# Two attention passes over one cache: lists of three early units in place of four, two units moved to each end, three rereads of a weight in place of four

## The chip, the cores and the metric

The kernel runs on one core of one Trainium2 chip. The metric is the device time of one launch in microseconds (us), the median over runs. Lower is better.

## The reference

Two blocks are applied one after the other, twice, to a decode step of eight rows (one token each), with the same weights and the same K and V caches both times:

```python
x = A_x
x = x + _A_ref(_layernorm(x), A_k_cache, A_v_cache, A_wq, A_wo)
x = x + _B_ref(_layernorm(x), B_w1, B_w2, B_w3, B_w4)
x = x + _A_ref(_layernorm(x), A_k_cache, A_v_cache, A_wq, A_wo)
x = x + _B_ref(_layernorm(x), B_w1, B_w2, B_w3, B_w4)

def _A_ref(x, k_cache, v_cache, wq, wo):      # B=8, D=448, 16 query heads, 8 kv heads, Sk=4096, Dh=256
    q = (x @ wq).reshape(B, Sq, Hq, Dh)
    scores = einsum("bhqd,bhkd->bhqk", q, repeat(k_cache, 2)) * Dh ** -0.5
    return einsum("bhqk,bhkd->bhqd", softmax(scores), repeat(v_cache, 2)).reshape(B, Sq, Hq * Dh) @ wo
```

With one token per row, the mixer inside `_B_ref` shifts everything out of the sequence, so of B there remain the norms, the two matrices w3 and w4 with a gelu between them, and the sums.

The caches are bf16, 128 MiB each. Everything else is small beside them.

## The kernel before

**Units, tiles and places.** The work of one pass, one row and one pair of kv heads is a unit, written (pass, row, pair): pass 0 or 1, rows 0 to 7, pairs 0 to 3. A unit has four K tiles and four V tiles of 1 MiB each. Tiles are loaded into 17 places of 1 MiB in SBUF. A K tile is turned in place by VectorE (three STREAM_TRANSPOSE, `transpose_k`, L897), then TensorE multiplies it with the query (`scores`, L904). Two tiles that lie in neighbouring places can be scored by one series of 256-wide matmuls (`also`), otherwise each has a series of 128-wide ones. A V tile needs 16 matmuls (`pv`, L978).

**What is read once and what twice.** Pairs 2 and 3 (`keep`) are "kept": once a row's pass 0 has used their tiles, they stay in the places, PSUM and a spare tile until the row's pass 1 has used them too. Pairs 0 and 1 (`free`) are read from HBM in each pass. Each row therefore has two free units in pass 0 and two in pass 1, 32 in all.

**Chains and lists.** Between a row's two passes lies a chain of small dependent steps (`chain`, L550): the output of pairs 2 and 3 times wo, norm, w3, gelu, w4, norm, the query of pass 1. While it runs, nearly all places hold the row's kept tiles, and three are left. To have something to do meanwhile, the plan takes free units of later rows out of their order (`ahead`, L624 to L628): their K tiles are turned and scored before the chain, and their V tiles are used under it. These V items are called `narrow`; the first twelve of a list are `halved`, that is, loaded as two DMAs of 512 KiB. A list has four units in rows 0, 1, 2 and 7 and three in rows 3 to 6. Row 0's own two free units of pass 0 come at the start (L700, L701), row 7's two of pass 1 at the end (L712, L713).

**The order.** `block`, `weights` and `first_kept` (L642 to L697) write the whole order of work by hand as a list of items: 527 of them, K (0), V (1) or weight (2). Within `block`, V items that are due are put between the K items. The main loop (L1113) walks the items. At each it issues the engines' work, then gives free places back and issues the next loads (`emit_loads`, L824) in the order of the items, on SyncE's queue, as far as places are free. Two K tiles of a `paired` unit (L744) are loaded by one 2 MiB DMA when two neighbouring places are free in time (`both_for`, L794).

**Generators.** The chain and the smaller jobs are Python generators that `step` (L1047) moves on by one yield at each item: of each of the kinds "chain", "last" and "rest", the oldest. While a chain runs under its narrow items (`alone`), other generators of the kinds "chain" and "last" wait. When a unit's output is complete, `half` (L504) scales it, copies it out of its PSUM bank, clears the bank and turns it into columns. There are two such banks (`free_o`). In pass 0 a row's pairs 0 and 1 go through one `half` (`first_half`, L545, kind "chain"); in pass 1 through `last` (L585, kind "last"), one for each unit if the two lie in different lists (`split`).

**Weights that are read again.** Half of wq (the heads of pairs 0 and 1) and half of wo have no lasting place. The wq half, 1.75 MiB in two places, is read at the start for all rows of pass 0 and then for pass 1 of the rows (0,3), (3,5), (5,7) and (7,8) (`q_rows`, L630). On its arrival TensorE makes the queries of those rows (`project_rows`, 64 matmuls, L350) and VectorE copies them. The wo half, 896 KiB, is read five times (`o_rows`, L631); `early_rows` (L599) multiplies the finished outputs of pairs 0 and 1 by it and adds the result to x. It first forces generators on until these outputs are there. At the last wo, `rest` does the second block of rows 0 to 3 for pass 1; rows 4 to 7 follow after the last V tile.

Of the kernel before, what the change touches and what calls it, by code (L numbers as in the profile page):

```python
# [17 lines left out]
def kernel(  # L18
# [521 lines left out]
    turned = {}  # L540

    def told(ps, b, gps):
        turned[ps, b] = turned.get((ps, b), 0) + len(gps)
# [55 lines left out]
    def early_rows(r0, r1, ps, slot):  # L599

        nb = r1 - r0
        for r in range(r0, r1):
            while turned.get((ps, r), 0) < (2, 4)[ps]:
                step(10 * len(items))
        y_ps = misc[:, 400 : 400 + 4 * nb].rearrange("p (f b) -> p f b", b=nb)
        run(
            add_cols(
                y_ps,
                lambda i: OT2[:, i % 2, i // 2, r0:r1],
                lambda i, at: wo_of(i, at, slot),  # L610
                range(NB2 // 2),
                4,
            )
        )
        xs = xT[:, :, r0:r1]
        nc.vector.tensor_add(xs, xs, y_ps)
# [15 lines left out]
    split = {  # L632
        (1, b)
        for b in range(Bn - 1)
        if any(sum((1, b, gp) in units for gp in free) == 1 for units in ahead)
# [6 lines left out]
    def block(k, v=None):  # L642

        fresh = [(number[v], 1, c) for c in range(4)] if v else []
        if k is None:
            due.extend(fresh)
            items.extend(due)
            due.clear()
            return
        number[k] = len(tasks)  # L650
        tasks.append(k)
        two = k[0] == 1 and k[2] in keep
        for c in range(4):
            items.append((number[k], 0, c))
            if two and c % 2 == 0:
                continue
            items.extend(due[:1])
            del due[:1]
            if c <= two:
                due.extend(fresh)  # L660
# [41 lines left out]
    o_rows[0] = (0, 1)  # L702
    first_kept(0, ahead[0], (0, 0, free[1]))
    for b in range(Bn):
# [39 lines left out]
    def paired(n, c):  # L744

        ps, _, gp = tasks[n]
        return gp in keep or tasks[n] in saved
# [365 lines left out]
    for idx, it in enumerate(items):  # L1113
# [10 lines left out]
        ps, b, gp = tasks[n]  # L1124
        if it == kept_q:
# [8 lines left out]
        if kv == 2:  # L1134
            rows = b
            if gp == "o" and rows is None:
                end_wo = slot
            elif gp == "o":
                early_rows(*rows, 0, slot)
                if rows[1] == Bn:  # L1140
                    assert pairs_done[1, MID - 1] == 4
                    early_rows(0, MID, 1, slot)
                    add_gen("rest", rest(), idx + 1, idx + 18, 20)
            elif c == 1:
# [3 lines left out]
                def q_of_block(c, fc):  # L1148
# [10 lines left out]
                    else misc[:, 352 : 352 + 2 * HH * nb]  # L1159
# [49 lines left out]
        else:  # L1209
# [12 lines left out]
            if final and gp in free:  # L1222
                pv_cols(oc, slot, c, gp, psv[slot_of[n]])
                if c % 2 == 1:
# [3 lines left out]
                    h0 = 8 * gp + 4 * u  # L1228
                    run(
# [9 lines left out]
            else:  # L1239
                g8 = gp // 2  # L1240
                if ("o", g8) not in st:
# [7 lines left out]
                if c == 0 and (alone_now or pairs_done.get((ps, b), 0) % 2 == 1):  # L1249
                    done = pairs_done[ps, b] + 1  # L1250

                    def ready(k=(ps, b), done=done):
                        return pairs_done[k] >= done

                    if ps == 0:
                        g = (first_half if done == 2 else chain)(b, st, ready)
                        add_gen("chain", g, main=done == 4)
# [196 lines left out]
```

## Time and profile before

| | |
|---|---|
| median of 3 runs | 1065.47 us (1064.1 to 1067.35) |
| the profiled execution | 1061.72 us |
| its span, first to last instruction | 1059.6 us |
| moved by DMA | 426.11 MB |
| busy: TensorE, VectorE, ScalarE, GpSimd | 59%, 58%, 15%, 2% of the span |

The profile is of one execution. Its page gives the busy time of each engine, the span in 40 slices, the DMA queues, the chain of work that ended last, groups of instructions by source line, and the DMA issues. Views of the trace cut out stretches of the span ("windows") or list the instructions in order of time; windows give, after the busy times, the granted clock, the busy share of the 16 DMA engines and the GB/s they moved. SPq is SyncE's DMA queue. In names such as `places<-places,qbd`, the left side is written and the right side read.

### The profile page before, as it was taken

The numbers are of one execution on the slowest core, as the hardware profiler recorded it, in microseconds if no ns is written. First come the engines' busy times: TensorE is split into PE (matmuls) and PEld (weight loads), VectorE is DVE, ScalarE is ACT, GpSimd is POOL, SyncE is SP. The second block draws the span as 40 slices with busy tenths as digits, with TensorE's granted clock in tenths as the row PEclk, the third lists the DMA queues.
The fourth block names the chain that finished last, engine by engine and source line by source line (L and its number), as shares of the span: only waits on it lengthen the run. The fifth ranks groups of instructions, "written<-read, shape, count | busy, mean of one in ns | idle before, by whom it ended". The sixth has DMA issues, their size and how long they took to land.

```text
span 1059.6 us, 29163 instructions
## 1 busy us (share of the span) xinstructions
PE 627.0 (59%) x12932; PEld 395.0 (37%) x12932; DVE 616.4 (58%) x1319; ACT 161.7 (15%) x613; POOL 16.4 (2%) x27
## 2 busy tenths in 40 slices
PE   3144457655575547664586566656764666657675
PEld 2022225432343324442343234423442444434455
DVE  5146862578527882467628952785288437792362
ACT  1011110211111111111112111111111111111110
POOL 0000000000000000000000000000000000000000
PEclk9999996665675656657656566656665686556665
DMA  9999999999999999999999999999999999999994
GB/s 300 387 424 424 424 415 388 422 421 423 401 406 426 424 420 404 409 403 424 414 389 426 425 410 410 378 425 412 401 424 423 393 389 420 423 418 348 393 416 203
DMA packets 71757, 426.11 MB, mean 402 GB/s; under 512 B 7496, under 2 KB 13520, under 8 KB 43856
## 3 DMA queue, kind: packets, MB, share of 16 engines
q1 hardware_dynamic: 71440, 424.01, 98.8%
q8 instruction: 101, 1.65, 0.6%
q10 hardware_dynamic: 192, 0.25, 0.1%
q14 instruction: 24, 0.20, 0.0%
HBM read 424.22 MB, written 0.01 MB: 400 GB/s over the span
## 4 chain that ended last, share of the span: by engine, by line
DMA 47%; DVE 24%; PE 21%; ACT 3%; issue 2%; SPq 2%; POOL 1%; DVEq 0%; ACTq 0%
DMA places<-in_A_v_cache_dram 25%; DMA places<-in_A_k_cache_dram 20%; DVE places L902 18%; PE sc L917 9%; PE o L986 7%; ACT p_n L926 2%; PE misc L174 2%; DMA places<-in_A_wq_dram 2%; PE misc L529 1%; DVE store L937 1%; DVE places L944 1%; DVE qbd L376 1%; SPq L193 1%; SPq L870 1%; ACT o_sb L523 1%
## 5 line engine op out<-in xcount | busy, mean ns | idle before, releaser
L902 DVE STREAM_TRANSPOSE places<-places 128x512 uint32<-128x512 uint32 (+1 forms) x576 | 455.5, 854 | 83.0 <-DMA places<-in_A_k_cache_dram 81.0
L917 PE MATMUL sc<-places,qbd 128*8 128x256 bf16 (+1 forms) x5024 | 246.9, 347 | 244.9 <-DVE places L902 236.1
L986 PE MATMUL o<-places,ptw 128*8 128x256 bf16 x3808 | 232.3, 369 | 101.4 <-DMA places<-in_A_v_cache_dram 70.9
L917 PEld LDWEIGHTS <-qbd 128*8 128x8 bf16 x5024 | 130.4, 104 | 327.8 <-DVE places L902 140.1
L986 PEld LDWEIGHTS <-ptw 128*8 128x8 bf16 x3968 | 103.7, 102 | 171.4 <-issue 95.8
L926 ACT ACTIVATE p_n<-sc 128x256 bf16<-128x256 f32 x128 | 95.4, 745 | 395.1 <-PE sc L917 392.4
L1108 ACT COPY ptw<-psv 128x32 bf16<-128x32 bf16 x248 | 52.6, 226 | 173.7 <-PE o L986 161.4
L976 ACT CAST psv<-misc 128x128 bf16<-128x128 f32 x64 | 17.0, 266 | 253.3 <-PE misc L969 253.3
L493 DVE RECIPROCAL rz<-misc 128x8 f32<-128x8 f32 (+1 forms) x35 | 6.7, 191 | 77.4 <-PE misc L490 77.4
L376 DVE CAST qbd<-misc 32x32 bf16<-32x32 f32 x128 | 23.2, 182 | 27.6 <-PE misc L370 26.3
L529 PE MATMUL misc<-R_t,o_sb 128*128 128x8 f32 (+1 forms) x132 | 26.7, 311 | 20.7 <-DVE R_t L515 13.9
L529 PEld LDWEIGHTS misc<-R_t,o_sb 128*128 128x128 f32 x132 | 23.8, 252 | 30.9 <-issue 17.2
L926 ACT ACTIVATION_READ_ACCUMULATOR p_n<-sc 128x1 f32 x128 | 33.8, 264 | 0.0
L174 PEld LDWEIGHTS <-w_sb 128*128 128x128 bf16 x896 | 27.3, 103 | 14.2 <-issue 13.8
L525 DVE MEMSET o<- 128x256 f32 x33 | 9.0, 272 | 35.0 <-PE o L986 31.2
L490 PE MATMUL misc<-zm,one 128*128 128x8 f32 (+1 forms) x70 | 17.1, 317 | 18.9 <-DVE zm L482 17.1
L275 POOL TENSOR_TENSOR t<-t,nhalf 128x2 f32<-128x2 f32 (+2 forms) x18 | 12.0, 670 | 957.7 <-DVE t L296 957.7
L490 PEld LDWEIGHTS misc<-zm,one 128*128 128x128 f32 x70 | 14.1, 251 | 29.1 <-issue 24.9
L969 PEld LDWEIGHTS <-p_n 128*128 128x128 bf16 x256 | 11.9, 105 | 31.6 <-issue 20.0
L969 PE MATMUL misc<-identb,p_n 128*128 128x32 bf16 x256 | 18.0, 190 | 9.3 <-ACT p_n L926 6.8
L937 DVE STREAM_TRANSPOSE store<-places 128x512 uint32<-128x512 uint32 x32 | 19.8, 686 | 0.0
L944 DVE STREAM_TRANSPOSE places<-store 128x512 uint32<-128x512 uint32 x32 | 19.7, 672 | 0.0
(150 smaller groups left out, 350.8 us busy)
## 6 DMA issues: line engine op xcount, KB each, us to landing
places<-in_A_k_cache_dram SPq DMA_DIRECT2D x62, 2048.0 KB, 17.5
places<-in_A_v_cache_dram SPq DMA_DIRECT2D x194, 512.0 KB, 7.2
places<-in_A_v_cache_dram SPq DMA_DIRECT2D x87, 1024.0 KB, 20.7
places<-in_A_k_cache_dram SPq DMA_DIRECT2D x68, 1024.0 KB, 13.3
places<-in_A_wq_dram SPq DMA_DIRECT2D x5, 1024.0 KB
rest<-in_A_v_cache_dram SPq DMA_DIRECT2D x8, 640.0 KB, 19.6
places<-in_A_wo_dram SPq DMA_DIRECT2D x5, 896.0 KB, 19.7
places<-in_A_v_cache_dram SPq DMA_DIRECT2D x8, 384.0 KB, 18.9
```

The source lines that it names most:

```text
L174: nc.tensor.matmul(bass.AP(out.tensor, out.offset, [out.ap[0], (1, WIDE)]), w, x.to_broadcast([128, WIDE]), start=start, stop=stop, skip_g ...
L376: nc.vector.tensor_copy(qbd[32 * a : 32 * a + 32, :, :, a, :], qs.rearrange("p e (f g u h) -> p (e f) u g h", f=2, u=2, h=2)[:, :, u],)
L490: nc.tensor.matmul(z_ps, ones, zm[:], start=True, stop=True)
L529: nc.tensor.matmul(ot_ps[:, j], o_sb[:].rearrange("p (i j) -> p j i", j=2)[:, j], R, start=True, stop=True)
L902: nc.vector.transpose(w, w)
L917: nc.tensor.matmul(sc[32 * k : 32 * k + 8, 128 * (x % 2) : 128 * (x % 2 + nx)], qbd[:, ep, gp % 2].rearrange("p a h -> p (a h)"), v, start ...
L926: nc.scalar.activation(p_sb[:, :, :, 2 * u : 2 * u + 2].rearrange("p t i x -> p x t i"), sc[:, 0:256].rearrange("p (x t i) -> p x t i", x= ...
L937: nc.vector.transpose(store[n][:].bitcast(U32), slot[:].bitcast(U32)[:, 512 * n : 512 * n + 512])
L944: nc.vector.transpose(slot[:].bitcast(U32)[:, 512 * n : 512 * n + 512], store[n][:].bitcast(U32))
L969: nc.tensor.matmul(pt_ps[:, t], p_sb[:, t].rearrange("p i x -> p (i x)"), cols, start=True, stop=True,)
L986: nc.tensor.matmul(o_ps[32 * q : 32 * q + 8, :], ptz[:, at : at + 8], v[:, y * Dh : (y + 1) * Dh] if v2 is None or y < PR else v2[:, (y - ...
L1108: nc.scalar.copy(ptw[:, ring_of[it], :, 6:8], psv[slot_of[it[0]]][:, it[2]])
```

## The change

- Every list has three units. The order of the free units starts with rows 1 to 6 of pass 0 and goes on with rows 0 to 5 of pass 1; 24 units lie in lists.
- Row 7's two free units of pass 0 follow row 0's at the start. Row 6's two of pass 1 stand before row 7's at the end, behind row 7's kept pairs.
- wq is read again for rows (0,4), (4,6) and (6,8). In the row where the list begins with a unit that needs the new queries (`at_once`, row 4), the reread stands ahead of it and the V items between its K items are spread further apart (`slow`).
- wo is still read five times, at rows 0, 1, 3, 5 and the end. `early_rows` now takes a range of heads, so that a row whose two units fell into different lists is served in two calls, the second half from the resident part of wo without a read (`o_late`, rows 2 and 4).
- `first_half` takes one or both units, since lists now split rows 2 and 5 in pass 0 and rows 1 and 4 in pass 1.
- The queries of a reread go to columns 192 and up of the PSUM tile `misc`, which were 352 and up.
- Ahead of the last row's products the program forces "last" generators to their end.

```diff
-    def first_half(b, st, ready):
-
-        yield from half(st["o", 0], st["z"], [0, 1], OT2[:, :, 0:HH, b], ready)
-        told(0, b, [0, 1])
+    def first_half(b, st, gps, ready):
+
+        o = st.pop(("o", 0))
+        yield from half(o, st["z"], gps, OT2[:, :, 4 * gps[0] : 4 * gps[-1] + 4, b], ready)
+        told(0, b, gps)
...
-    def early_rows(r0, r1, ps, slot):
+    def early_rows(h0, h1, r0, r1, ps, slot):
 
         nb = r1 - r0
-        for r in range(r0, r1):
-            while turned.get((ps, r), 0) < (2, 4)[ps]:
-                step(10 * len(items))
+        while not {(ps, r, h // 4) for r in range(r0, r1) for h in range(h0, h1)} <= turned:
+            assert gens
+            step(10 * len(items))
...
-                range(NB2 // 2),
+                range(2 * h0, 2 * h1),
...
-    order = [(0, b, gp) for b in range(1, Bn) for gp in free]
-    order += [(1, b, gp) for b in range(Bn - 1) for gp in free]
-    ahead = []
-    for n in (4, 4, 4, 3, 3, 3, 3, 4):
-        ahead.append(order[:n])
-        del order[:n]
-    assert len(ahead) == Bn and not order
-
-    q_rows = {3: (0, 3), 5: (3, 5), 7: (5, 7), Bn: (Bn - 1, Bn)}
-    o_rows = {1: (1, 3), 3: (3, 7), 7: (7, 8)}
+    ends = (6, 7)
+    order = [(0, b, gp) for b in range(1, Bn - 1) for gp in free]
+    order += [(1, b, gp) for b in range(ends[0]) for gp in free]
+    ahead = [order[3 * b : 3 * b + 3] for b in range(Bn)]
+    assert len(order) == 3 * Bn
+
+    q_rows = {4: (0, 4), 6: (4, 6), Bn: (6, 8)}
+
+    o_rows = {
+        0: [(0, 8, 0, 1), (0, 8, 7, 8)],
+        1: [(0, 4, 1, 3), (4, 8, 1, 2)],
+        3: [(0, 4, 3, 6), (4, 8, 3, 5)],
+        5: [(0, 8, 6, 7)],
+    }
+    o_late = {2: (4, 8, 2, 3), 4: (4, 8, 5, 6)}
...
-            if two and c % 2 == 0:
+            if (two or slow) and c % 2 == 0:
+                if slow and c == 0:
+                    due.extend(fresh)
                 continue
...
-        ready = b < Bn - 1
-        if b in q_rows and not ready:
+        at_once = b in q_rows and todo[0][1] >= q_rows[b][0]
+        if at_once:
+            block(k2, before)
             weights("q", q_rows[b])
-        block(todo.pop(0), before)
-        if b in q_rows and ready:
-            weights("q", q_rows[b])
-        if len(todo) > 2:
-            block(todo.pop(0))
-        if b in o_rows:
-            weights("o", o_rows[b])
-        block(k2)
-        block(todo.pop(0), k2)
-        if todo:
-            block(todo.pop(0))
+            if b in o_late:
+                o_late_at[len(items)] = o_late[b]
+            block(todo.pop(0), k2, True)
+        else:
+            block(todo.pop(0), before)
+            if b in q_rows:
+                weights("q", q_rows[b])
+            if b in o_rows and b:
+                weights("o", o_rows[b])
+            if b in o_late:
+                o_late_at[len(items)] = o_late[b]
+            block(k2)
+            if not b:
+                weights("o", o_rows[b])
+            block(todo.pop(0), k2)
+        while todo:
+            block(todo.pop(0), None, at_once)
...
-    o_rows[0] = (0, 1)
-    first_kept(0, ahead[0], (0, 0, free[1]))
+    block((0, Bn - 1, free[0]), (0, 0, free[1]))
+    block((0, Bn - 1, free[1]), (0, Bn - 1, free[0]))
+    first_kept(0, ahead[0], (0, Bn - 1, free[1]))
...
             weights("q", q_rows[Bn])
-            block((1, b, free[0]), k2)
-            block((1, b, free[1]), (1, b, free[0]))
-            weights("o", None)
-            block(None, (1, b, free[1]))
+            before = k2
+            for k in [(1, r, gp) for r in range(*q_rows[Bn]) for gp in free]:
+                block(k, before)
+                if before == k2:
+                    weights("o", None)
+                before = k
+            block(None, before)
...
-        return gp in keep or tasks[n] in saved
+        return gp in keep or tasks[n] in saved or tasks[n][:2] == (1, ends[0])
...
+        if idx in o_late_at:
+            early_rows(*o_late_at[idx], 0, None)
...
-                    else misc[:, 352 : 352 + 2 * HH * nb]
+                    else misc[:, 192 : 192 + 2 * HH * nb]
...
+                    while any(e["kind"] == "last" for e in gens):
+                        step(10 * len(items))
```

More of the change, by code (lines that the diff above doesn't have):

```diff
@@ L538 @@
     free_o = list(o_banks)
[L540 removed]
+    turned = set()
     def told(ps, b, gps):
[L543 to L548 removed]
+        turned.update((ps, b, gp) for gp in gps)
+    def first_half(b, st, gps, ready):
+        o = st.pop(("o", 0))
+        yield from half(o, st["z"], gps, OT2[:, :, 4 * gps[0] : 4 * gps[-1] + 4, b], ready)
+        told(0, b, gps)
     def chain(b, st, ready):
@@ L621 @@
     assert Bn > 2 and free == [0, 1] and GP == 4
-    order = [(0, b, gp) for b in range(1, Bn) for gp in free]
-    order += [(1, b, gp) for b in range(Bn - 1) for gp in free]
-    ahead = []
-    for n in (4, 4, 4, 3, 3, 3, 3, 4):
-        ahead.append(order[:n])
-        del order[:n]
-    assert len(ahead) == Bn and not order
-    q_rows = {3: (0, 3), 5: (3, 5), 7: (5, 7), Bn: (Bn - 1, Bn)}
-    o_rows = {1: (1, 3), 3: (3, 7), 7: (7, 8)}
+    ends = (6, 7)
[5 more added lines that the diff above has]
+    o_rows = {
[4 rows of a table added]
+    }
+    o_late = {2: (4, 8, 2, 3), 4: (4, 8, 5, 6)}
+    o_late_at = {}
     split = {
-        (1, b)
-        for b in range(Bn - 1)
-        if any(sum((1, b, gp) in units for gp in free) == 1 for units in ahead)
+        (ps, b)
+        for ps in range(2)
+        for b in range(Bn)
+        if any(sum((ps, b, gp) in units for gp in free) == 1 for units in ahead)
     }
@@ L658, in block @@
             del due[:1]
-            if c <= two:
+            if c <= two and not slow:
                 due.extend(fresh)
@@ L1137 @@
                 end_wo = slot
+                early_rows(0, HH, 0, MID, 1, slot)
+                add_gen("rest", rest(), idx + 1, idx + 18, 20)
             elif gp == "o":
[L1139 to L1143, printed above, removed]
+                for who in rows:
+                    early_rows(*who, 0, slot)
             elif c == 1:
@@ L1240 @@
                 g8 = gp // 2
-                if ("o", g8) not in st:
+                if c == 0 and ("o", g8) not in st:
                     while not free_o:
@@ L1249 @@
                 if c == 0 and (alone_now or pairs_done.get((ps, b), 0) % 2 == 1):
-                    done = pairs_done[ps, b] + 1
+                    done = pairs_done.get((ps, b), 0) + 1
                     def ready(k=(ps, b), done=done):
-                        return pairs_done[k] >= done
+                        return pairs_done.get(k, 0) >= done
                     if ps == 0:
-                        g = (first_half if done == 2 else chain)(b, st, ready)
-                        add_gen("chain", g, main=done == 4)
+                        if done == 4:
+                            add_gen("chain", chain(b, st, ready), main=True)
+                        else:
+                            add_gen(
+                                "chain", first_half(b, st, [gp] if alone_now else free, ready)
+                            )
                     elif done == 2:
```

2 lines of the change are left out of this document (1 added, 1 removed).

## The prediction

> **What bounds the kernel now.** First the page: engines, slices, queue.
>
> ```profile
> PE 627.0 (59%) x12932; PEld 395.0 (37%) x12932; DVE 616.4 (58%) x1319; ACT 161.7 (15%) x613; POOL 16.4 (2%) x27
> DMA  9999999999999999999999999999999999999994
> GB/s 300 387 424 424 424 415 388 422 421 423 401 406 426 424 420 404 409 403 424 414 389 426 425 410 410 378 425 412 401 424 423 393 389 420 423 418 348 393 416 203
> DMA packets 71757, 426.11 MB, mean 402 GB/s; under 512 B 7496, under 2 KB 13520, under 8 KB 43856
> ```
>
> No engine is busy for 60% of the span, and the DMA engines are busy in every slice but the last. Slices come back to 424 to 426 GB/s and never go higher: that is the full rate here. So the kernel is bound by its loads, and the question is which bytes go and where the rate sags. 426.11 MB at 424 GB/s would take 1005.0 us of the 1059.6. I then cut windows: two stretches at the full rate, then the eight stages from a list's first V item to the first kept V item of pass 1, row by row.
>
> ```profile
> 55.00:85.00 30.00, 14.96 (x298) 9.09 (x298) 15.71 (x28) 2.91 (x12) 0.00 (x0) 1.00 1.01 426
> 100.00:140.00 40.00, 16.59 (x312) 9.43 (x308) 31.12 (x48) 5.63 (x19) 0.00 (x0) 1.00 1.01 424
> ```
>
> ```profile
> 158.70:209.30 50.60, 36.23 (x728) 23.78 (x731) 19.14 (x63) 7.57 (x32) 1.26 (x2) 0.66 1.02 405
> 284.00:333.40 49.40, 33.11 (x695) 21.81 (x695) 19.18 (x64) 7.53 (x32) 1.25 (x2) 0.71 1.01 406
> 404.40:454.80 50.40, 35.46 (x724) 22.73 (x724) 19.14 (x64) 7.53 (x32) 1.25 (x2) 0.66 1.02 406
> 523.90:563.40 39.50, 30.60 (x592) 18.99 (x595) 11.20 (x50) 6.11 (x25) 1.26 (x2) 0.62 1.01 399
> 626.00:666.00 40.00, 28.11 (x620) 18.61 (x619) 11.28 (x50) 5.87 (x25) 1.25 (x2) 0.71 1.02 405
> 734.00:774.80 40.80, 28.20 (x620) 18.70 (x619) 13.68 (x54) 5.91 (x25) 1.25 (x2) 0.71 1.02 405
> 836.40:876.90 40.50, 27.39 (x652) 19.01 (x651) 11.26 (x50) 5.83 (x25) 1.25 (x2) 0.79 1.01 385
> 960.00:1015.20 55.20, 38.12 (x853) 25.76 (x852) 19.56 (x66) 7.40 (x32) 1.25 (x2) 0.62 0.98 379
> ```
>
> I price a window by what it lost against the full rate: its length times (1 - GB/s / 424). Rows 0 to 7 lose 2.27, 2.10, 2.14, 2.33, 1.79, 1.83, 3.72 and 5.86 us, together 22.0. Lists of four (rows 0 to 2) and of three (rows 3 to 5) lose alike. Rows 6 and 7 stand out; each has a wq reread inside. Next come the four rereads and the K stretches (turning K tiles, ahead of a list's V items) of rows 6 and 7.
>
> ```profile
> 454.00:460.00 6.00, 3.82 (x99) 2.86 (x98) 3.07 (x6) 1.00 (x4) 0.00 (x0) 0.66 1.07 338
> 664.00:680.00 16.00, 10.80 (x241) 6.61 (x234) 10.31 (x18) 3.21 (x14) 0.00 (x0) 0.61 0.98 352
> 864.00:870.00 6.00, 4.30 (x124) 3.22 (x121) 1.62 (x8) 2.17 (x7) 0.00 (x0) 0.97 1.05 346
> ...
> 994.00:1000.00 6.00, 3.40 (x53) 2.11 (x53) 2.45 (x8) 0.80 (x3) 0.00 (x0) 0.50 1.03 318
> ```
>
> ```profile
> 802.10:836.40 34.30, 18.38 (x338) 9.77 (x342) 25.66 (x38) 6.24 (x22) 0.00 (x0) 0.55 1.01 418
> 925.00:960.00 35.00, 22.05 (x450) 13.38 (x454) 28.57 (x49) 6.42 (x24) 0.54 (x1) 0.50 1.00 407
> ```
>
> The rereads lose 1.22, 2.72, 1.10 and 1.50 us beside their bytes; row 6's K stretch loses 0.49 and row 7's 1.40. Why row 7 is late shows on VectorE, in order of time:
>
> ```profile
> 880.41 0.27 DVE L358 CAST qT<-misc 128x16 bf16<-128x16 f32 x2 [5.88 <-PE misc L350]
> ...
> 903.51 0.16 DVE L616 TENSOR_TENSOR xT<-xT,misc 128x4 f32<-128x4 f32 x1 [2.00 <-PE misc L174]
> 905.61 0.17 DVE L616 TENSOR_TENSOR xT<-xT,misc 128x16 f32<-128x16 f32 x1 [1.94 <-PE misc L414]
> ```
>
> ```profile
> 937.64 15.14 DVE L902 STREAM_TRANSPOSE places<-places 128x512 uint32<-128x512 uint32 x20
> ```
>
> Within 26 us it stands idle 9.8 us, for the reread's queries and for two wo products, with 24 K tiles to turn. A K tile costs it 3 transposes, 15.14 / 20 x 3 = 2.27 us, against 2.47 us for 1 MiB of DMA, so over K tiles alone it hardly catches up. The V items start late, give their three places back late, and DMA starves: its busy share is 0.98 in row 7's stage.
>
> **The change, part by part.**
>
> *One reread less.* 1.75 MiB are 1.835 MB, 4.33 us at 424 GB/s; no place or engine has to give anything for it. Its sag goes too, somewhere between 1.10 and 2.72.
>
> *Where the other three fall.* By its order of items, the reread for (0,4) has ten loads out, itself among them, before the next place comes free; I give it the 1.22 of the first row. That for (4,6) has eight, with two K tiles behind it, just like the one at 664 us: 2.72. That for (6,8) is issued under row 7's list as the third one now is under row 6's, so row 7's stage gets row 6's 3.72. Ahead of it row 7 turns 20 K tiles in place of 24, with no reread and no wo product among them, and `rest` comes only at the end: its K stretch gets row 6's 0.49.
>
> *Lists of three.* Lists in rows 0 to 3 now hold units of pass 0, whose outputs queue behind the chain. Today only row 3 is such a list of three: 2.33 each. Rows 4 to 6 get 1.8. Stages, separate rereads and last K stretch are today 22.04 + 1.22 + 2.72 + 1.40 = 27.4, and then 4 x 2.33 + 3 x 1.8 + 3.72 + 1.22 + 2.72 + 0.49 = 22.9. That is 4.5 us, which holds the sag and row 7's lateness; bounds 1.3 (the lateness of 3.2, below, comes back elsewhere) and 6.7 (rows 0 to 3 come down to row 4's 1.79).
>
> *Units at both ends.* 16 MiB move to each end, K and V tiles in turn, so VectorE has 4.9 us for each 2.27. The loads of the weights at the start are as they were. At the end the last eight V tiles come one per 2.47 us, and this stands unchanged behind them:
>
> ```profile
> 1029.74 18.36 DMA places<-in_A_v_cache_dram
> ...
> 1056.37 0.27 DVE places L1419
> ```
>
> From the last landing at 1048.1 to the end of the span are 11.5 us before and after. Row 6's last `half` has to be done by the second of these eight tiles, six tiles (15 us) ahead of the end, and `rest` earlier still.
>
> *What is added.* The instruction lists of the two builds differ by this: 128 wo matmuls more (448 for 320) in ten calls for five; two more `half`; 20 tiles more that are scored alone, since their places aren't neighbours; 11 K loads of 2 MiB fewer and 22 of 1 MiB more.
>
> ```profile
> L917 PE MATMUL sc<-places,qbd 128*8 128x256 bf16 x3168 | 182.0, 386 | 182.6 <-DVE places L902 180.2 <-DVE places L962 1.3 <-DVE zs_t L479 0.6
> L917 PE MATMUL sc<-places,qbd 128*8 128x128 bf16 x1856 | 64.9, 280 | 62.3 <-DVE places L902 55.8 <-ACT p_n L926 5.3 <-DVE zs_t L479 0.5
> L523 ACT COPY o_sb<-o 128x256 f32<-128x256 f32 x33 | 12.7, 384 | 17.8 <-PE o L986 17.6
> 933.77 0.33 SPq L839 DMA_DIRECT2D places<-in_A_k_cache_dram  x1
> ```
>
> Wo: 64 matmuls keep VectorE idle 1.94 to 2.00 us (rows above), so 128 are 3.9. Scores: 640 narrow matmuls at 64.9 / 1856 = 35.0 ns less 320 wide ones at 182.0 / 3168 = 57.4 ns, 4.0 us of TensorE. A `half` holds a copy of 0.38 us and no DMA; I call it 2 us with its matmuls, two are 4 (an estimate). Together 11.9 us if all lay open, nothing if all is hidden. TensorE and VectorE, idle over 40% of the span while DMA isn't, cover it; the present calls lie in stretches that still move 418 to 420 GB/s. So I take a value near nothing, 0.8. Loads: 1 MiB loads run at 426 GB/s (55 to 85 us, where none is paired), paired ones at 424 (100 to 140 us), so nothing; the open bound is SyncE's 0.33 us an issue, 11 x 0.33 = 3.6.
>
> The Trainium skill, "DMA: Bandwidth & Descriptors", section "Anatomy of one DMA — SWDGE (gpsimd) path", speaks against this edit: it fits each DMA with a fixed 2.0 us beside its bytes. By that the 11 additional DMAs would cost 22 us, an estimate from that page, which would end at 1079. The page fits single DMAs on another issue path; the 426 GB/s row has many on the queue and shows no such cost.
>
> *The sum.* 4.3 + 4.5 - 0.8 = 8.0 us. The profiled execution took 1061.72 us, 2.1 more than its span, and should come to 1053.7. It is itself 3.75 below the median of the three runs; the median should go from 1065.47 to **1057.5 us**.
>
> **The rivals.**
>
> *Late V items in the early rows (slower).* Row 7's lateness is worth 5.86 - 1.50 - 2.10 = 2.3 us in its stage and 1.40 - 0.49 = 0.9 ahead of it, 3.2 together. In the changed kernel wo products stand in the K stretches of rows 1 to 5, two calls each in rows 1 and 3, and forced generators ahead of them. If each of these rows starts its V items as late as row 7 does, that is 5 x 3.2 = 16 us, and the time 1065.5 - 8.0 + 16 = 1073.5. It decides from the third such row (8.0 / 3.2 = 2.5). For it: the idle rows at 903 and 905 us. Against: rows 1 and 3 have a wo call now, of 64 matmuls, and their stages run at 406 and 399; a row's two calls there become two of 32, as much in sum; and each row has 20 K tiles to turn at most, with eight V loads between and behind them that give VectorE 8 x 2.47 = 20 us.
>
> *The lateness moves with a reread.* Row 4's or row 6's K stretch behind its reread takes what row 7's loses: 1057.5 + 3.2 = 1060.7. For it: the 5.88 us of idle VectorE. Against: the second reread has such a stretch behind it now, and the stage that follows runs at 405.
>
> *The bytes aren't the bound where they are saved.* If after each list the chain sets the time and loads only fill it, the 4.3 us and the sag come back as waiting for places, and row 7's 3.2 and less remain: about 1063 to 1066. For it: 0.98 at 664 us. Against: the busy share is 1.01 or more in seven of the eight stages.
>
> *More issues cost.* 3.6 us by the bound above: 1061.1. Against: the 426 GB/s.
>
> **How the numbers follow.** A measurement of this kernel can't tell less than about 0.3% from no change, so the borders are 1062.3 and 1068.7. The forecast has 0.60, with a range of its own from 1053 (bounds 6.7 and nothing added) to 1061 (4 of the 11.9 open). The late V items have 0.17; a part of it, with two or three late rows, would be no change. The moved lateness has 0.13, the bytes that don't count 0.08, the issues 0.02. Faster: 0.58 + 0.10 + 0.01 + 0.02 = 0.71. No change: 0.02 + 0.03 + 0.06 + 0.03 = 0.14. Slower 0.15. The range goes from 1051 (1.5 us of the runs' spread below 1053) to 1068, which leaves out most of the late rows.
>
> **What would show it.** Right: 424.3 MB moved; a span with three sags of the reread in place of four; row 7's stage at about 385 GB/s and the one before it at 418; stages of some 40 us at 399 to 406 in all other rows; about 11.5 us from the last V landing to the end. Wrong: stages of rows 1 to 5 below 390 GB/s with a busy share under 1.00, V items that wait for VectorE or an output bank rather than for DMA, or a K stretch under 410 behind the rereads of rows 4 and 6. Should the last V tiles have landed well before their products, the end would be bound by engines and the forecast for another reason too low.

## The result, and the profile after

| | median | runs |
|---|---|---|
| before | 1065.61 us | 10, 1063.77 to 1068.58 |
| changed | 1061.86 us | 10, 1059.44 to 1064.14 |

The ratio is 0.996 (95% interval 0.9948 to 0.9971): 3.75 us or 0.4% faster. The direction and the range held; the forecast gain was 8.0. Both profiled executions take the same time, though: 1061.44 us for the changed kernel (span 1059.3), 1061.72 for the one before. The latter lies below all ten timed runs of its kernel, so it flatters the kernel before by almost the whole gain. Stages of the changed kernel are therefore compared below over several traces, and gains by ratios; the kernel before has only this one trace.

The changed kernel's page: its slices, and what its DMA moved.

```profile
GB/s 303 389 420 424 422 420 420 394 416 423 418 388 416 420 415 332 409 423 419 395 394 420 421 377 410 423 421 404 377 424 422 392 417 422 419 398 392 418 418 187
DMA packets 72768, 424.32 MB, mean 401 GB/s; under 512 B 7608, under 2 KB 13632, under 8 KB 43456
```

The 1.8 MB are gone, but the mean rate has not risen with it: 401 GB/s, where it was 402. One slice stands out, the 16th with 332 GB/s, around 411 us. The windows of the changed kernel, cut as before: its eight stages from a list's first V item to the first kept one of pass 1, rows 0 to 7. (Columns as before: length, busy time of the engines, granted clock, busy share of DMA, GB/s.)

```profile
189.00:228.90 39.90, 27.61 (x592) 18.30 (x593) 13.72 (x54) 5.88 (x25) 1.26 (x2) 0.74 1.02 401
293.20:334.20 41.00, 28.26 (x652) 19.16 (x651) 11.27 (x50) 5.92 (x25) 1.25 (x2) 0.71 1.01 395
398.80:441.50 42.70, 31.19 (x652) 20.47 (x651) 13.68 (x54) 5.95 (x25) 1.25 (x2) 0.58 0.97 361
504.80:545.50 40.70, 28.50 (x592) 18.29 (x595) 11.13 (x50) 5.97 (x25) 1.25 (x2) 0.71 1.01 401
613.00:654.60 41.60, 28.72 (x589) 18.72 (x589) 13.69 (x54) 5.95 (x25) 1.25 (x2) 0.71 1.01 388
718.00:758.00 40.00, 27.65 (x588) 18.34 (x587) 11.27 (x50) 5.92 (x25) 1.25 (x2) 0.75 1.02 404
825.60:867.00 41.40, 28.63 (x624) 19.34 (x627) 13.73 (x54) 5.92 (x25) 1.25 (x2) 0.66 1.02 403
927.40:968.60 41.20, 28.61 (x656) 19.76 (x659) 11.28 (x50) 5.97 (x25) 1.25 (x2) 0.75 1.02 390
...
894.20:927.40 33.20, 18.21 (x334) 9.91 (x335) 25.39 (x38) 6.23 (x23) 0.00 (x0) 0.55 1.01 418
545.50:577.50 32.00, 20.44 (x458) 12.79 (x462) 26.63 (x46) 4.36 (x17) 0.00 (x0) 0.55 1.02 401
758.00:780.00 22.00, 14.31 (x326) 8.95 (x330) 17.74 (x34) 3.47 (x15) 0.00 (x0) 0.66 0.99 381
```

Priced as in the prediction, length times (1 - GB/s / 424), the stages lose 2.2, 2.8, **6.3**, 2.2, **3.5**, 1.9, 2.0 and 3.3 us, 24.3 in all, where 18.4 were forecast. The last K stretch (894 us) loses 0.47, forecast 0.49. The two rereads outside the stages (546 and 758 us) lose 1.7 and 2.2, forecast 1.22 and 2.72. So in this trace the miss lies in row 2 and, less, in row 4. From the last landing, at 1029.43 + 18.41 = 1047.84 (the chain of waits), to the end are 11.5 us, as forecast:

```profile
1029.43 18.41 DMA places<-in_A_v_cache_dram
```

What makes row 2 late shows on VectorE just ahead of its K stretch, in order of time (the bracket has the idle time before, and what ended it):

```profile
326.68 0.45 DVE L983 STREAM_TRANSPOSE places<-sc 128x256 uint32<-128x256 uint32 x1 [1.73 <-ACT p_n L947]
327.05 0.67 DVE L983 STREAM_TRANSPOSE places<-store 128x512 uint32<-128x512 uint32 x1
327.65 2.47 DVE L965 STREAM_TRANSPOSE places<-store 128x512 uint32<-128x512 uint32 x4
330.04 0.17 DVE L493 RECIPROCAL rz<-misc 128x8 f32<-128x8 f32 x1
330.25 0.17 DVE L515 TENSOR_TENSOR R_t<-rz,fold 128x8 f32<-128x8 f32 x1
...
335.41 0.77 DVE L376 CAST qbd<-misc 32x32 bf16<-32x32 f32 x4 [3.59 <-PE misc L370]
336.21 1.25 DVE L923 STREAM_TRANSPOSE places<-places 128x1024 uint32<-128x1024 uint32 x1
```

and on TensorE at the same time:

```profile
325.73 0.39 PE L490 MATMUL misc<-zm,one 128*128 128x8 f32 x2
330.56 0.99 PE L529 MATMUL misc<-R_t,o_sb 128*128 128x8 f32 x4 [4.45 <-DVE R_t L515]
331.48 1.88 PE L938 MATMUL sc<-places,qbd 128*8 128x256 bf16 x32
334.24 0.59 PE L1007 MATMUL o<-places,ptw 128*8 128x256 bf16 x6 [0.87 <-ACT ptw L1129]
334.41 0.85 PE L1007 MATMUL o<-rest,ptw 128*8 128x256 bf16 x10
335.04 0.26 PE L370 MATMUL misc<-qT,identb 128*32 128x16 bf16 x2
```

Two waits follow each other. First a `half` has begun (its sum, L490), and its next steps on VectorE (L493, L515) stand behind 3.6 us in which VectorE turns the tiles parked in PSUM back (L983, L965). TensorE, whose work runs in its order here, stands for 4.45 us at its matmul L529, and the kept pair's scores come behind it. Then VectorE waits 3.59 us for the query of the next unit (L376): row 2's list starts with (0,4,0), which begins a new row, and its query's matmuls (L370) stand on TensorE behind those scores and the first V product. Only then comes the first K tile. In the K stretch a wo product follows as a third wait. Ahead of rows 4 and 6 the same two waits occur (541 and 754 us). The lists of rows 1, 3, 5 and 7 start with the second unit of a row, its query is there, and only the first wait occurs.

### The profile page after: what moved, and what is told of

Read it like the earlier page. It is cut to its first block, busy times and chain, and to the rows that moved or that the text cites. A ratio compares the mean times of both kernels' runs of the same rounds, so it can differ in the third digit from the quotient of the medians.

```text
span 1059.3 us, 29997 instructions
## 1 busy us (share of the span) xinstructions
PE 632.2 (60%) x13328; PEld 401.6 (38%) x13328; DVE 617.0 (58%) x1334; ACT 161.3 (15%) x615; POOL 16.3 (2%) x27
## 4 chain that ended last, share of the span: by engine, by line
DMA 46%; DVE 26%; PE 21%; ACT 3%; issue 2%; SPq 1%; POOL 1%; DVEq 0%; ACTq 0%
DMA places<-in_A_v_cache_dram 30%; DVE places L923 20%; DMA places<-in_A_k_cache_dram 13%; PE sc L938 7%; PE o L1007 6%; PE misc L174 3%; ACT p_n L947 2%; DMA places<-in_A_wq_dram 2%; DVE store L958 2%; PE misc L529 1%; DVE qbd L376 1%; DMA places<-in_A_wo_dram 1%; DVE places L965 1%; SPq L193 1%; PE misc L350 0%
## 5 line engine op out<-in xcount | busy, mean ns | idle before, releaser
L938 PEld LDWEIGHTS <-qbd 128*8 128x8 bf16 x5344 | 134.8, 103 | 319.0 <-DVE places L923 140.8
L493 DVE RECIPROCAL rz<-misc 128x8 f32<-128x8 f32 (+1 forms) x37 | 6.8, 183 | 89.0 <-PE misc L490 89.0
L529 PE MATMUL misc<-R_t,o_sb 128*128 128x8 f32 (+1 forms) x140 | 29.8, 322 | 40.7 <-DVE R_t L515 35.4
L529 PEld LDWEIGHTS misc<-R_t,o_sb 128*128 128x128 f32 x140 | 26.9, 268 | 51.0 <-issue 40.4
L376 DVE CAST qbd<-misc 32x32 bf16<-32x32 f32 x128 | 23.3, 182 | 37.1 <-PE misc L370 35.6
L174 PEld LDWEIGHTS <-w_sb 128*128 128x128 bf16 x896 | 27.1, 100 | 16.5 <-issue 15.8
L174 PEld LDWEIGHTS <-wo_sb 128*128 128x128 bf16 x704 | 20.9, 100 | 6.4 <-issue 6.4
L965 DVE STREAM_TRANSPOSE places<-store 128x512 uint32<-128x512 uint32 x32 | 19.7, 674 | 0.0
L174 PE MATMUL misc<-xb,w_sb 128*128 128x32 bf16 x448 | 16.1, 187 | 4.9 <-DVE xb L304 4.8
## 6 DMA issues: line engine op xcount, KB each, us to landing
rest<-in_A_v_cache_dram SPq DMA_DIRECT2D x8, 640.0 KB, 18.4
```

The source lines that it names most:

```text
L174: nc.tensor.matmul(bass.AP(out.tensor, out.offset, [out.ap[0], (1, WIDE)]), w, x.to_broadcast([128, WIDE]), start=start, stop=stop, skip_g ...
L376: nc.vector.tensor_copy(qbd[32 * a : 32 * a + 32, :, :, a, :], qs.rearrange("p e (f g u h) -> p (e f) u g h", f=2, u=2, h=2)[:, :, u],)
L529: nc.tensor.matmul(ot_ps[:, j], o_sb[:].rearrange("p (i j) -> p j i", j=2)[:, j], R, start=True, stop=True)
L938: nc.tensor.matmul(sc[32 * k : 32 * k + 8, 128 * (x % 2) : 128 * (x % 2 + nx)], qbd[:, ep, gp % 2].rearrange("p a h -> p (a h)"), v, start ...
L965: nc.vector.transpose(slot[:].bitcast(U32)[:, 512 * n : 512 * n + 512], store[n][:].bitcast(U32))
```

## The experiments

All times are medians, and the ratio is to the kernel before, run beside it on the same chip. Where two ratios are compared, their intervals are combined.

| run | median | ratio, 95% interval |
|---|---|---|
| changed | 1061.86 | 0.9960 (0.9948 to 0.9971) |
| changed, once more | 1061.14 | 0.9942 (0.9919 to 0.9964) |
| next query early | 1057.25 | 0.9933 (0.9917 to 0.9948) |
| half first | 1054.46 | 0.9908 (0.9893 to 0.9923) |
| both | 1057.30 | 0.9905 (0.9882 to 0.9928) |
| row 2's wo product left out | 1057.65 | 0.9936 (0.9920 to 0.9953) |
| row 3's wo products left out | 1060.93 | 0.9945 (0.9919 to 0.9971) |
| two more products in row 1 | 1063.43 | 0.9975 (0.9961 to 0.9989) |
| two more products in row 2 | 1064.16 | 0.9997 (0.9984 to 1.0009) |
| half first, two more in row 2 | 1060.71 | 0.9959 (0.9944 to 0.9975) |
| half first, products behind the K stretch | 1056.25 | 0.9908 (0.9890 to 0.9926) |
| a fourth reread | 1065.97 | 1.0011 (1.0001 to 1.0022) |
| before, half first | 1062.20 | 0.9960 (0.9941 to 0.9980) |

The changed kernel was measured twice, and its two ratios differ by 0.18%, within their intervals. Gains and costs below are counted from the first, 0.9960; counted from the second, each gain is 1.9 us smaller and each cost 1.9 us larger.

**The next query early.** Under pass 1's scores of pair 3, the query for the next loaded K tile is spread (the `...` stands for three lines that keep account of the rows whose queries exist):

```diff
...
+            if (ps, gp, c) == (1, keep[1], 1):
+                m = next((tasks[i[0]] for i in items[idx + 1 :] if i[1] == 0 and not here(i)), None)
+                who = m and (m[0], m[1], m[2] // 2)
+                if who and who not in q_of and (m[0] == 0 or (m[2] in free and m[1] in asked)):
+                    give_q(who)
             if (ps, gp, c) == (1, keep[0], 1):
```

> The changed kernel, with one edit: the query of the next unit whose K tiles are loaded is spread (four matmuls, four copies) right after the first scores of the row's kept pair 3 in pass 1, not after the first V product of pass 1. Nothing is left out. Theory Q: in rows 2, 4 and 6 the list begins a new row, so its query must be spread first, and today VectorE stands idle 3.6 us for it (331.8 to 335.4 us in the changed kernel's trace) and turns the first K tile some 4 us later than in the odd rows; the lateness is still there at row 2's V items, whose stage loses 6.5 us (361 GB/s). Then the first transposes of rows 2, 4 and 6 come some 4 us earlier, row 2's stage rises to 390 to 405 GB/s and row 4's from 387 to 400, and the time goes from 1061.9 to 1056 to 1058.5. Rival W (the wo products in the K stretches make the V items late): the first transposes come earlier but the stages of rows 2 and 4 stay below 390 GB/s, and the time stays at 1061 to 1062.5. Rival R (the sag in row 2 is chance of one execution): the stage rises, the median of the runs doesn't: 1061 to 1062.5.

The median falls by 0.27% of the kernel before, some 3 us (0.8 to 4.9), to 1057.25; counted from the second measurement it is 0.09%, not clear of nothing. VectorE now goes from the parked tiles straight on (first row), and row 2's stage (second row; another view, windows) rises from 361 to 396 GB/s:

```profile
333.11 4.15 DVE L923 STREAM_TRANSPOSE places<-places 128x1024 uint32<-128x1024 uint32 x5
```

```profile
396.80:438.30 41.50, 29.17 (x654) 20.00 (x654) 13.70 (x54) 5.96 (x25) 1.25 (x2) 0.66 1.02 396
```

The first transpose is 3.1 us earlier, and row 2's stage loses 2.7 us for 6.3; row 4's rises to 400. That is theory Q, and W falls. R (chance of one execution) falls with the other traces of the changed kernel, below, more than with this time.

**Half first.** A begun `half` is forced to its end before the parked tiles are turned back:

```diff
             if (ps, gp, c) == (1, keep[0], 1):
+                while locked:
+                    step(10 * len(items))
                 where[(b, part[0]), part[1:]] = part_place
```

> The changed kernel, with one edit: a half that has begun is forced to its end before VectorE turns the tiles parked in PSUM back into their places in pass 1. Nothing is left out. In the changed kernel's trace such a half's matmul waits 4.45 us for a VectorE copy that stands behind this 3.6 us of turning back (326.7 to 330.6 us), and the scores of the kept pair 2 stand behind the matmul; in all, TensorE waits 35.4 us for it, against 13.9 us in the kernel before. Theory S: this wait, new in rows 0 to 2, makes the K stretches late; without it K tiles are turned up to 4 us earlier in every row and the time falls by 2 to 4, to 1058 to 1060. Theory Q (the query stands behind TensorE's order in rows 2, 4, 6 alone): it helps rows 2, 4 and 6 as far as the V product comes earlier, so row 2's stage rises somewhat, and in the other rows nothing changes in GB/s: 1059.5 to 1061.5. Rival W (wo products): 1061 to 1062.5.

1054.46 us, 0.52% of before below the changed kernel's ratio, 5.5 us (3.5 to 7.6): more than either theory gave. Counted from the second measurement it is 3.6 us (0.7 to 6.5), still a gain, and within theory S. Who waited for R_t, first in the changed kernel, then with this edit (us, times):

```profile
  PE misc L529: 35.4, 8
  DVE qT L533: 7.5, 9
  DVE OT L533: 2.3, 6
```

```profile
  DVE qT L533: 3.0, 9
  DVE o L525: 1.1, 1
  DVE OT L533: 1.0, 2
```

TensorE's eight waits are gone. Row 2's first transpose comes 2.3 us earlier (VectorE, in order of time), its stage runs at 389 (windows):

```profile
333.10 0.77 DVE L376 CAST qbd<-misc 32x32 bf16<-32x32 f32 x4 [0.81 <-PE misc L370]
333.90 3.56 DVE L923 STREAM_TRANSPOSE places<-places 128x1024 uint32<-128x1024 uint32 x4
```

```profile
397.00:435.10 38.10, 29.23 (x656) 19.98 (x659) 11.09 (x50) 5.91 (x25) 1.25 (x2) 0.63 1.01 389
...
609.70:646.30 36.60, 27.05 (x592) 17.99 (x595) 11.05 (x50) 5.98 (x25) 1.25 (x2) 0.78 1.02 406
```

Against the first trace of the changed kernel rows 2 and 4 account for 3.2 and 2.0 us (6.3 to 3.1, and 3.5 to 1.6), against the mean of four traces (below) for 2.4 and 0.9; the other stages don't gain clearly. Of theory S the wait is right, but not that every row wins by it. Row 2's first tile is turned 0.8 us later here than with the early query, and its stage loses no less (3.1 beside 2.7), yet the time is 0.25% lower: that part of the gain isn't row 2's, and no trace shows where it is.

**Both edits.**

> The changed kernel with both edits: the next query spread early and a begun half forced to its end before the parked tiles are turned back. Nothing is left out. Theory T (lateness counts only above what three free places cover, so any one cure suffices where one stage is late): no more than the better edit alone, 1053 to 1055. Rival (each microsecond of waiting on TensorE or VectorE costs a microsecond): the gains of about 3.5 and 6.2 us add up, 1050 to 1051.5.

The ratio is that of the better edit alone, 0.9905 beside 0.9908, and 3.8 us below the changed kernel run beside it (next). Added up, the two gains would give 0.9881, just outside the interval, so that they don't add up is likely rather than shown. The median of 1057.3 is above the forecast, but the kernel before took 1066.3 beside it.

**The changed kernel once more.**

> The changed kernel once more, to be timed beside the next ones and to see in a second trace which stages' losses repeat. If row 2's stage is late by its order of work, it loses 4 us or more again; if it was chance, 2 to 3. Time 1059.5 to 1062.

The stages of rows 0, 2 and 4 in the second trace (windows):

```profile
189.70:231.40 41.70, 29.68 (x588) 18.96 (x587) 13.65 (x54) 6.02 (x25) 1.26 (x2) 0.66 1.00 386
...
400.40:442.30 41.90, 28.49 (x652) 19.72 (x651) 13.64 (x54) 5.86 (x25) 1.25 (x2) 0.70 0.95 368
...
613.30:654.00 40.70, 28.65 (x588) 18.53 (x587) 13.68 (x54) 5.91 (x25) 1.25 (x2) 0.70 1.02 400
```

Row 2 loses 5.5 again, row 4 only 2.3; row 0 loses 3.7, for 2.2 in the first trace. Two other experiments leave the order up to row 2 untouched (the fourth reread, row 3's products) and lose 4.8 and 5.2 there. Row 2 is late by its order, 5.5 us in the mean of these four; row 4 varies, 1.6 to 3.5, and so does row 0, 2.2 to 3.7.

**Row 2's wo product left out** (32 matmuls and one sum, so that row 2 lacks a part of its first attention output).

```diff
-    o_late = {2: (4, 8, 2, 3), 4: (4, 8, 5, 6)}
+    o_late = {4: (4, 8, 5, 6)}
```

> The changed kernel without row 2's late wo product in pass 0: 32 matmuls and one sum are left out, so that row 2 lacks a part of its first attention output. Rival W (wo products make row 2's V items late): VectorE's 1.55 us of idle time at 347 us goes, row 2's stage rises from 361 to 380 GB/s or more, and the time falls by 1.5 to 4. Theory Q: the lateness is 10 us before that product and 13 after it, so 1 to 2 us of it go, row 2's stage gets at most 1.5 us shorter: 1060 to 1062.

```profile
399.40:439.40 40.00, 27.70 (x652) 19.37 (x651) 13.67 (x54) 5.84 (x25) 1.25 (x2) 0.70 1.00 383
```

Row 2's stage rises to 383 GB/s and loses 3.9, less than in any of the four traces, and the time falls by 0.24%, some 2.6 us (0.4 to 4.7). That is what rival W gave, not theory Q, by which the stage would get at most 1.5 us shorter (it gets 2.7). Counted from the second measurement the time falls by 0.06%, which is nothing clear. So the stage speaks for the product as a third cause of the same lateness; the time alone doesn't secure it.

**Row 3's wo products left out** (64 matmuls and two sums; rows 3, 4 and half of 5 lack that part).

```diff
-        3: [(0, 4, 3, 6), (4, 8, 3, 5)],
+        3: [],
```

> The changed kernel with the wo bytes of row 3 loaded as ever, but their two products (64 matmuls, two sums) left out, so that rows 3, 4 and half of 5 lack a part of their first attention output. Row 3's V items aren't late in the trace (2.2 us lost in its stage). Theory T: VectorE's idle time for them goes and DMA gains nothing, 1060 to 1062, as the changed kernel; row 3's stage stays at 2 to 3 us lost. Rival W (each wo call in a K stretch costs its idle time): 2 to 4 us less, 1057 to 1059.

1060.93 beside 1061.14, run in one set: nothing, and the spread of the runs leaves some 1.4 us, less than rival W's 2 to 4. Twice the matmuls of the run above, and no gain; row 3's stage isn't late (401 GB/s). This fits theory T: a product costs only where lateness has already used up the cover, that is, the loads that three free places still let through.

**Two more products in row 1, and in row 2.** The same product twice more, copied aside (shortened, and as in row 2; in row 1 the rows are 1, 2).

```diff
+        if (h0, h1, r0, r1, ps) == (4, 8, 2, 3, 0):
+            for _ in range(2):
+                run(add_cols(...))
+                aside = chn.tile([128, 16], FP32, tag="aside")
+                nc.vector.tensor_copy(aside[:, 0 : 4 * nb].rearrange("p (f b) -> p f b", b=nb), y_ps)
```

> The changed kernel with two more wo products in row 1's K stretch, made from the same data and put aside unused: 64 matmuls and two copies, some 2.8 us of idle VectorE. The result is the same. Row 1 turns its first K tile 6 us after its landing, row 2 its first one 10 us after. Theory T (lateness costs DMA time only beyond what is made up again and three places cover): 0 to 1 us more than the changed kernel, 1061 to 1062; row 1's stage loses 2 to 3.5. Rival A (each idle microsecond of VectorE in a K stretch costs one): 2.5 to 3 more, 1063.5 to 1064.5.

> The changed kernel with the same two additional products in row 2's K stretch, beside its wo product there. Theory T: row 2 is already late at its V items, so nothing covers them: 2 to 3.5 us more than the changed kernel, 1063 to 1065, and row 2's stage loses 7.5 to 9. Rival A: 2.5 to 3 more as well, so the two are told apart by the run with row 1. Rival R (row 2's loss has another cause, not VectorE's lateness): 0 to 1 more, 1061 to 1062.

The stages of rows 1 and 2 with the products in row 1:

```profile
293.60:335.30 41.70, 29.08 (x652) 19.84 (x651) 11.27 (x50) 5.93 (x25) 1.25 (x2) 0.66 1.01 394
400.20:442.20 42.00, 29.19 (x656) 20.15 (x659) 13.75 (x54) 5.98 (x25) 1.25 (x2) 0.66 0.95 355
```

and row 2's K stretch and stage with them in row 2:

```profile
369.00:403.70 34.70, 19.16 (x350) 10.60 (x345) 27.26 (x44) 7.05 (x26) 0.00 (x0) 0.55 0.96 391
```

```profile
403.70:446.20 42.50, 28.79 (x652) 19.79 (x651) 13.67 (x54) 5.86 (x25) 1.25 (x2) 0.66 0.94 350
```

In row 2 they cost 0.37% (0.9997 against 0.9960), 3.9 us: the stage now loses 7.4 and the K stretch ahead of it 2.7 (0.8 in the changed kernel), where DMA's busy share is already 0.96. That fits theory T, and A too, and excludes R. In row 1 the stage itself loses no more than before (3.0), as T has it, but row 2's loses 6.8 and the time rises by 0.15%, 1.6 us, between what T and A gave. Between the two placements lie 0.7 us of the medians, 0.22% of the ratios. Taken alone the run with row 1 decides nothing.

**Half first, with two more products in row 2; and half first, with the products behind the K stretch.** The latter moves the `o_late` calls from ahead of pair 2's K tiles to ahead of pair 3's V items.

> The changed kernel with a begun half forced to its end before the parked tiles are turned back (the best so far, some 6 us faster than the changed one), and the two additional products in row 2's K stretch. Theory T: the half taken forward gave row 2 some 4 us, which the products use up again in part: 0 to 2 us more than without them, 1055 to 1057.5, row 2's stage at 3 to 5. Rival A: 2.5 to 3 more, 1057 to 1058.

> The changed kernel with a begun half forced to its end before the parked tiles are turned back, and the wo products of the second half of rows 2 and 5 moved behind the K stretch, ahead of the V items of pair 3. Nothing is left out. Theory T: no row is late any more, so little is left to win: 0 to 1 us less than with the first edit alone, 1054 to 1056.5. Rival A: 1.5 us per product, 3 less, 1051.5 to 1053.

The second gains nothing over half first, as theory T says; A's 3 us less lie outside the intervals. The first fits neither T (0 to 2 us more) nor A (2.5 to 3): its row 2 stage covers the products (386 GB/s, 3.3 us lost, as without them),

```profile
399.60:436.90 37.30, 27.56 (x656) 19.41 (x658) 11.07 (x50) 5.97 (x25) 1.25 (x2) 0.72 0.99 386
```

yet the ratio is 0.9959 and not 0.991, 5.4 us (2.9 to 8.0) that are in no single stage of its trace. Its losses are a few tenths of a microsecond higher in most stages, also in those whose order is the same. What does this was not found.

**A fourth reread.**

```diff
-            weights("q", q_rows[Bn])
+            weights("q", (6, 7))
...
+                if k == (1, 7, free[0]):
+                    weights("q", (7, 8))
```

> The changed kernel with a fourth reread of wq put back: rows 6 and 7 have one each at the end, the second ahead of row 7's K tiles. Nothing is left out. It prices one reread by itself. The prediction's term: 4.3 us for 1.835 MB and a sag of 1.1 to 2.7, so 1061.9 + 5.4 to 7.0 = 1067.3 to 1069, at 426.1 MB. Rival (bytes that aren't the bound): less than 2 us, 1062 to 1064. If only the bytes count and the sag is hidden by the many loads that are out at the end: 1066.2.

0.51% of before above the changed kernel: 5.4 us, the lower end of the forecast 5.4 to 7.0, at 426.18 MB. The ends of the two intervals leave 3.2 to 7.9, which excludes the rival's 2. Bytes are the bound even at the end.

**The kernel before, half first.**

> The kernel before with the edit that gave most on the changed one: a begun half is forced to its end before the parked tiles are turned back. In the trace of before that wait of TensorE is there four times (13.9 us in all), in the changed kernel eight times (35.4 us). Nothing is left out. Theory N (the change brought the wait into rows where nothing covers it): a gain of 0 to 2 us, 1062.5 to 1064.5. Rival O (an old wait that costs the kernel before as much): 4 us or more, 1058.5 to 1060.5.

Theory N (0 to 2) falls, if narrowly: the kernel before gains 0.4%, 4.3 us (2.1 to 6.3), by the same edit. Its row 7 shows where a part of it comes from (K stretch and stage):

```profile
921.30:956.20 34.90, 20.98 (x447) 12.93 (x447) 28.65 (x49) 6.38 (x24) 0.55 (x1) 0.56 1.01 417
956.20:1013.40 57.20, 38.52 (x852) 25.76 (x852) 19.52 (x66) 7.46 (x32) 1.24 (x2) 0.64 1.01 393
```

They lose 0.6 and 4.2 where they lost 1.4 and 5.9, so 2.5 us of row 7's lateness, in one trace each. Between the cured kernels the change is worth 0.9960 - 0.9908, 0.52% or 5.5 us (2.9 to 8.2), about what one reread costs by itself.

## Why the prediction was right, and where it was off

The time fell into the range, and the bytes were priced rightly; of the gain in the stages nothing is left on balance. At the medians, the time less the 2.1 us beside the span and less the bytes at 424 GB/s leaves 58.5 us lost before (1065.61 - 2.1 - 1005.0) and 59.0 changed (1061.86 - 2.1 - 1000.8). The 4.2 us of bytes were gained; the 4.5 us of smaller losses were made, in part, and lost again in other rows.

- **Bound by the loads; one reread less.** Right. The term was 4.3 us and a sag of 1.1 to 2.7; a reread put back costs 5.4, which would make the sag 1.1, but its interval of 3.2 to 7.9 holds any of these. 5.4 is more than the whole measured gain.
- **Where the other three rereads fall.** Right in sum: 1.7 and 2.2 us for 1.22 and 2.72, and 3.3 for 3.72 in row 7's stage.
- **Row 7's lateness goes.** Right: its K stretch loses 0.47 (forecast 0.49), and its stage 3.3, 3.7 in the mean of four traces (forecast 3.72).
- **Lists of three in rows 0 to 3 at 2.33 us each.** This step failed. In the mean of four traces rows 0, 1 and 3 came to 3.0, 2.5 and 2.3, but row 2 to 5.5: 3.2 us more. The price was taken from row 3 of the kernel before, the only list of three with units of pass 0, but other work stood ahead of its K stretch. There, too, a new row's query was waited for (2.36 us), but the parked tiles had been turned back before the half's sum was ready (before, VectorE, in order of time), so that TensorE had no such wait for R_t, and a reread of wq followed:

```profile
439.18 2.46 DVE L944 STREAM_TRANSPOSE places<-store 128x512 uint32<-128x512 uint32 x4
...
442.88 0.17 DVE L515 TENSOR_TENSOR R_t<-rz,fold 128x8 f32<-128x8 f32 x1
445.40 0.77 DVE L376 CAST qbd<-misc 32x32 bf16<-32x32 f32 x4 [2.36 <-PE misc L370]
```

  In row 2 of the changed kernel the half behind the parked tiles, the query and the wo product add up. Each of the three, taken away alone, brings half of the excess back or more: 2.7, 3.1 and 3.9 us lost in place of 5.5, each in one trace. Rows 4 and 6 have the first two waits as well and lose 2.5 and 1.6; a reread stands behind them there, and that it gives VectorE time to catch up is argued, not shown.
- **Row 4 at 1.8** was too low as well: 2.5 in the mean of the same four traces, and so was row 5 with 2.5.
- **The slower rival, late V items in the early rows,** thus did take place, but clearly in one row where it needed three to decide, and of the three waits it had named only the wo product. That row 2's excess equals its price of 3.2 us is chance.
- **What is added, 0.8.** The price of more DMAs near nothing was right, but the row it rests on was misread. In the kernel before, three K loads issued from 44 to 60 us are of 2 MiB (first row, DMA issues in that stretch), and the one whose landing the view gives took 25.0 us, so that paired loads run between 55 and 85 us too. In the changed kernel the K and V loads up to 84 us are all of 1 MiB (second and third row, issues from 25 to 84 us), and 55 to 85 us move 420 GB/s (last row, windows):

```profile
places<-in_A_k_cache_dram SPq DMA_DIRECT2D x3, 2048.0 KB, 25.0
```

```profile
places<-in_A_k_cache_dram SPq DMA_DIRECT2D x11, 1024.0 KB, 19.9
places<-in_A_v_cache_dram SPq DMA_DIRECT2D x11, 1024.0 KB, 19.8
```

```profile
55.00:85.00 30.00, 15.99 (x362) 9.93 (x361) 16.26 (x29) 3.07 (x13) 0.00 (x0) 1.00 1.01 420
```

  Against 424 GB/s that is 0.02 us per MiB, some 0.5 us for the 22 loads of 1 MiB that the change adds (an estimate from these rows). So the fixed 2 us per DMA from the Trainium skill, "DMA: Bandwidth & Descriptors", section "Anatomy of one DMA — SWDGE (gpsimd) path", has no place on this queue. The products aren't of one price: nothing in row 3, 2.6 us for 32 matmuls in row 2, as far as that is secured.
- **The sum against its own time.** The profiled execution of before was 3.75 us below its median, and the sum carried this offset over to the median. The two profiled executions of the changed kernel lie only 0.4 and 1.0 below theirs. At 1061.44 and 1060.18 us they miss the 1053.7 that the sum gave for such an execution by 7.7 and 6.5; the eight stages account for 5.9 and 5.5 of it. That the medians miss by only 4.3 is therefore in part luck. An execution of before at its median lost more than this trace shows; no trace says where.
- **The forecast's own range** has a slip: bounds of 6.7 with nothing added give 1057.5 - 2.2 - 0.8 = 1054.5, not 1053.

What the stages leave open, 1.8 and 1.0 us, lies in part behind row 7's stage, where the two traces lose 15.8 and 14.7 to the end of the span and the kernel before 14.2 (350 GB/s over 90.7 us, 354 over 89.2, 288 over 44.4). Stages differ by 1 us and more from trace to trace.

## What to carry to other kernels

A kernel that is bound by its loads can be priced by cutting its span at the places where few buffers are free and weighing each window by its lost rate; such terms carried over to about a microsecond in seven of eight stages. A stage from which a price is taken has to be the same in what its engines do ahead of it: here a half whose next step stood behind other work on VectorE held TensorE, and a query behind that held VectorE. In most of these runs lateness cost little until the buffers' cover was used up, so several small waits in one place are worth looking for together, and curing one of them can be enough; the two products that cost 5.4 us behind a cure don't fit this. Forcing the begun half ahead of the parked tiles, the best version here, is 0.9% faster than the kernel before.

## What the runs showed that was not expected

- The edit that takes away 35.4 us of TensorE's waits in eight places gained about 5.5 us, of which rows 2 and 4 hold 3.3 to 5.2; the kernel before, with four such waits of 13.9 us in all, gained 4.3.
- Two additional products that their row's stage covers nevertheless came with 5.4 us more over the whole kernel, spread thinly over stages of the same order of work. This stays open.
